# First expert slot of a routed layer cut into parts of 128 and 224 rows, with the narrow part's second layer turned

## Chip, core and metric

The kernel runs on one core of a Trainium2 chip. The metric is device time in microseconds (us), the median of several executions. The engines named below are TensorE (PE; PEld is its weight load, which overlaps PE), VectorE (DVE), ScalarE (ACT), GpSimd (POOL) and SyncE (SP), which issues most DMAs.

## Reference

Three blocks follow each other: local plus pooled attention, a routed layer with one expert per token, and a dense layer with a piecewise quadratic activation. The change touches the second block only.

```python
# x: attention output, 2304 tokens x 512
logits = x @ w_gate                     # 8 experts
expert_idx = np.argmax(logits, axis=1)  # one expert per token
for e in range(8):
    mask = expert_idx == e
    h = np.maximum(x[mask] @ w1[e], 0.0)        # 512 -> 1024
    out[mask] = gate_w[mask, None] * (h @ w2[e])  # 1024 -> 512
# then: h = out @ w_in; g = quadratic(h); result = g @ w_out   (512 -> 2048 -> 512)
```

All of it is to come out in float32 precision. The kernel therefore splits each operand into a rounded high part (`hi`, `wh`, `hh`, `xh`) and the rest (`lo`, `wl`, `hl`, `xl`), and each product is the sum of three passes: high by high, high by low, low by high.

## The kernel before, in words

Attention, gating and the scattering of the tokens to a DRAM table by expert (`xs_d`) come first and follow an order written out by hand (`ORDER`). Then eight *slots* run one after the other, the fullest expert first. A slot has 8 steps `f`, one for each 128 of the 1024 hidden features. A step has two products. `emit_p1` (the first product) has one weight block of 128 features stationary and the tokens as moving columns, and leaves a 128 x tokens block of hidden values in PSUM; ACT applies ReLU and rounds (`hh`), DVE makes the rest (`hl`). `emit_p2` (the second product) adds that block's share to four PSUM banks `y0` to `y3`, each holding 128 of the 512 outputs by tokens; its stationary operand is again a weight block and the tokens move. Each product of a full slot is 12 matmuls. The program emits the first product of step f+1 ahead of the second of step f.

Slot 0 has room for 416 tokens, but its expert is known before all tokens are scattered: the first rows of that expert are loaded early (`ld_rows`). So slot 0 starts with a *part A* of 144 tokens, while the rest of the routing is still being worked out. In A the first product is 4 matmuls of 288 columns (`hi` and `lo` of the tokens side by side) and 4 of 144. A runs steps 0 to 5; then the other tokens are fetched, turned (`x_rest`) and split; *part B*, the other 208 (or up to 272) tokens, runs steps 0 to 5 with the same weights; then all tokens run steps 6 and 7 together, 352 columns wide. `by_count` picks the narrow form (352 tokens in all) by the expert's count, and the traced execution took it. I write A0, B0 and so on for steps of the parts.

Weights come in tiles of 128x1024: tile 2j holds the first layer's weights of steps 2j and 2j+1, tile 2j+1 those of the second layer. SP loads a tile into one of four raw buffers (`load_wt`, issued by `wload`, L172), ACT rounds it to `wh` (`whi`, L181), DVE makes `wl` (`wlo`, L185), and that frees the raw buffer. For part A these three are placed by hand: `wh_`, `wd_` and `load_wt`, `wd_` inside `emit_p1` (its argument `mid`). From then on `next_wt` converts the next tile and issues the load of another one when the table `WFIRST` says how many tiles should be converted after sequence step k. A transfer that SP must wait for blocks all that stand behind it on SP. `blank_rows` makes SP wait for a flag that `tables` computes on DVE; `load_rest` fetches the other tokens of slot 0; `load_x(1)` those of slot 1, whose transposes (`xT_parts`) stand on PE in two halves ahead of the last two second products of slot 0. `starts`, `positions` and `emit_places` are bookkeeping on DVE that must run somewhere in slot 0.

Of the kernel before, what the change touches and what calls it, by code (L numbers as in the profile page):

```python
# [9 lines left out]
F32 = mybir.dt.float32  # L10
# [3 lines left out]
AF = mybir.ActivationFunctionType  # L14
ALU = mybir.AluOpType
# [4 lines left out]
B, H, S, D = 4, 8, 576, 64  # L20
# [12 lines left out]
CAP = 384  # L33
# [3 lines left out]
YCOLS = NT + CAPS[0]  # L37
NEG = -8.0e9
NWB, NWC, NWR = 3, 4, 4
NA, GA, FA, TOP = 144, 3, 6, 4096  # L40
NWT = NWB + NWC
NGR = 4
CONV0 = 8
WSTEP = (2, 1, 2, 1, 1, 1, 0, 0)
WFIRST = (0, 0, 0, 6, 6, 7, 8, 9, 10, 11, 11, 12, 13, 14)
PAT_MIN = float(np.array(0x38100000, np.uint32).view(np.float32))

C_ID = 0
# [72 lines left out]
def body(ctx: ExitStack, tc: tile.TileContext, qT, kT, kD, vS, wg, w1, w2, w_in, w_out, cst, out, dbg=None, parts="all"):  # L121
    nc = tc.nc
    PE, ACT, DVE, POOL, SP = nc.tensor, nc.scalar, nc.vector, nc.gpsimd, nc.sync
# [11 lines left out]
    def bank(tag):  # L135
        return ps.tile([128, 512], F32, tag=tag, name=tag)
# [3 lines left out]
    def next_bank(tag):  # L140
        turn[tag] += 1
        return bank(f"{tag}{turn[tag] % 2}")

    ident = const.tile([128, 128], F32, tag="ident", name="ident")
# [21 lines left out]
    wcount = [0]  # L166
# [37 lines left out]
    wts, wsrc, wpend = {}, [(s, k // 2, k % 2) for s in range(E) for k in range(8)], []  # L204

    def load_wt(after=None):
        if wsrc:
            s, j, second = wsrc.pop(0)
            if s < E:
                src, shp = slot_src(s, j, second)  # L210
            else:
                src, shp = w_out_src(wout_s, j) if second else w_in_src(win_s, j)
            wpend.append((s, wload(src, shp, after)))
# [44 lines left out]
    held = {}  # L258
# [391 lines left out]
    first = {}  # L650
# [60 lines left out]
    def wd_(eng, i):  # L711
        wlo(eng, *first["w", i])
# [188 lines left out]
    hb, yb = [None, bank("s1")], []  # L901
# [14 lines left out]
    for j in range(F2 // 256):  # L916
        for c in range(2):
            src = (w_in.bitcast(I32) if wide else w_in)[256 * c:256 * c + 256, :]
            n = 512 if wide else 256
# [100 lines left out]
    def split_psum(src, n, func_relu, hi, lo):  # L1020

        if func_relu:
            ACT.activation(out=hi, in_=src, func=AF.Relu)  # L1023
            DVE.scalar_tensor_tensor(out=lo, in0=src, scalar=0.0, in1=hi.bitcast(F32), op0=ALU.max, op1=ALU.subtract)  # L1024
        else:
            ACT.copy(out=hi, in_=src)
            DVE.tensor_tensor(out=lo, in0=src, in1=hi.bitcast(F32), op=ALU.subtract)
# [23 lines left out]
    def x_rest():  # L1051
        xr, m = first["xr"], (CAPS[0] - 128 - NA) // 2
        n = CAPS[0] - NA
        for c in range(4):
            p_ = next_bank("o")
            for t, c0, k in ((0, 0, 128), (2, 128, m), (3, 128 + m, m)):
                PE.transpose(out=p_[:, c0:c0 + k], in_=xr[0:k, t, 128 * c:128 * c + 128], identity=ident[0:k, 0:k])
            hi, lo = first["x"][c]
            split_psum(p_[:, 0:n], n, False, hi[:, NA:], lo[:, NA:])
            if c % 2:  # L1060
                yield

    PASSES = ((0, 0), (0, 1), (1, 0))

# [9 lines left out]
    def emit_p1(v, f, xhl, mid=None):  # L1074
        s, b, cap, _ = part(v)
        h_ps = hb[(f + 1) % 2]
        w = wts[s][2 * (f // 2)]

        def products(b, m):
            n = 0  # L1080
            for wi, xi in PASSES if f else (PASSES[0], PASSES[2], PASSES[1]):
                for c in range(4):
                    o = 256 * c + 128 * (f % 2)
                    PE.matmul(out=h_ps[:, b:m], lhsT=w[wi][:, o:o + 128], rhs=xhl[c][xi][:, b:m],  # L1084
                              start=(n == 0), stop=(n == 11))
                    n += 1

        hi = hp.tile([128, CAPS[0]], F32R, tag="hh", name="hh")
        lo = hp.tile([128, CAPS[0]], F32R, tag="hl", name="hl")
        if v == "A":  # L1090
            hv = h_ps[:, 0:2 * NA].rearrange("p (i n) -> p i n", i=2)
            for i in range(2):
                for c in range(4):
                    o = 256 * c + 128 * (f % 2)
                    PE.matmul(out=hv[:, 0] if i else hv, lhsT=w[i][:, o:o + 128], rhs=xhl[c][:, 0] if i else xhl[c],
                              start=(i == 0 and c == 0), stop=(i == 1 and c == 3))
            t = hp.tile([128, CAP], F32, tag="r", name="r", bufs=2)[:, 0:NA]
            ACT.copy(out=t, in_=hv[:, 1])
            DVE.tensor_tensor(out=t, in0=hv[:, 0], in1=t, op=ALU.add)
            ACT.activation(out=hi[:, 0:NA], in_=t, func=AF.Relu)  # L1100
            if mid is not None:
                wd_(DVE, mid)
                if mid > 2:
                    load_wt()
            DVE.scalar_tensor_tensor(out=lo[:, 0:NA], in0=t, scalar=0.0, in1=hi[:, 0:NA].bitcast(F32), op0=ALU.max, op1=ALU.subtract)
            return hi, lo
        by_count(v, products)
        split_psum(h_ps[:, b:cap], cap - b, True, hi[:, b:cap], lo[:, b:cap])
        return hi, lo

    def emit_p2(v, f, hl, y_ps):
        w = wts[part(v)[0]][2 * (f // 2) + 1]

        def products(b, m):
            for c, i in hi_first(4, 1):
                wi, xi = PASSES[i]
                o = 512 * (f % 2) + 128 * c
                PE.matmul(out=y_ps[c][:, b:m], lhsT=w[wi][:, o:o + 128], rhs=hl[xi][:, b:m],  # L1118
                          start=(f == 0 and i == 0 and v not in ("A", "B")), stop=(f == 7 and i == 1))

        by_count(v, products)

# [65 lines left out]
    def clear(t, stop):  # L1188
        PE.matmul(out=t[:, 0:CAPS[0]], lhsT=onesb, rhs=zerob.to_broadcast([128, CAPS[0]]), start=True, stop=stop)
# [2 lines left out]
    hl = emit_p1("A", 0, xhl, 2)  # L1192
    hb[0] = bank("s0")
    clear(hb[0], True)
    seq = [("A", f) for f in range(FA)] + [("B", f) for f in range(FA)] + [(0, f) for f in range(FA, 8)]
    for k, (v, f) in enumerate(seq):
        if k == FA - 1:
            xb = x_rest()
            next(xb)
            emit_p2(v, f, hl, yb)  # L1200
            next(xb)
            xhl = first["x"]
            hln = emit_p1(*seq[k + 1], xhl)
        elif k + 1 < len(seq):
            hln = emit_p1(*seq[k + 1], xhl, k + 2 if 0 < k < 4 else None)
            if f == 6:
                xTs = xT_parts(sx)
                next(xTs)
            if k == 0:
                yb.extend(bank(f"y{c}") for c in range(4))  # L1210
                for t in yb:
                    clear(t, False)
            emit_p2(v, f, hl, yb)
        else:
            next(xTs)
            emit_p2(v, f, hl, yb)
            emit_y(0, yb)
            xhl = next(xTs)
            sx = load_x(2)
            hln = emit_p1(1, 0, xhl)  # L1220
        hl = hln
        if k < 3:
            wh_(k + 3)
        while k > 2 and wcount[0] < WFIRST[k] and wpend:
            next_wt()
        if k == 0:
            tables()
            blank_rows()
            load_rest()
            load_wt()  # L1230
        elif k == FA - 2:
            load_n(0)
            starts()
        elif k == FA - 1:
            positions()
            actx.close()
            rest_pools()
            for c in range(4):
                POOL.memset(yT[c][:, NT:], 0.0)
        elif k == FA:  # L1240
            inner_pools()
            for c in range(4):
                for i, copy in enumerate((ACT.copy, POOL.tensor_copy)):
                    copy(out=first["x"][c][i][:, 0:NA], in_=first["xa"][c][:, i])
        elif k == FA + 3:
            sx = load_x(1)
        if k == len(seq) - 3:
            load_off(0)
            load_n(1)
        if 7 <= k < 14:  # L1250
            emit_places(k - 7)
    for e in range(1, E):
        y_ps = yb
        for f in range(8):
# [195 lines left out]
```

## Time and profile before

| | us |
|---|---|
| median of 3 executions | 760.73 (758.19 to 761.08) |
| profiled execution, its own time | 756.73 |
| its span in the trace | 755.0 |
| first matmul of part A to first matmul of slot 1 | 116.64 to 160.34 |
| PE busy over the span | 731.9 (97%) |

The profile gives the busy time of each engine, the waits with what ended them, a timeline with the start of each group of instructions, and the DMA issues. The start-to-start distance of matmuls in the timeline is what one costs when PE is full; the duration of one is longer, because they are pipelined.

### The profile page before, as it was taken

How to read it: one execution, taken by the hardware profiler on the slowest of the kernel's cores; microseconds unless marked ns; L12 is line 12 of the kernel's file. 1: busy time of each engine (PE TensorE's matmuls, PEld its weight loads, DVE VectorE, ACT ScalarE, POOL GpSimd, SP SyncE). 2: the span in 40 equal slices, each digit the busy share in tenths (PEclk: the TensorE clock that was granted, in tenths of full speed). 3: DMA queues.
4: the chain of work that ended last, by engine and by line, in shares of the span. 5: the costliest groups of instructions: out<-in, count | busy, mean ns of one | idle time of the engine just before them, and what ended most of it. 6: DMA issues, size and time to landing. Idle time of an engine off the chain costs nothing.

```text
span 755.0 us, 14570 instructions
## 1 busy us (share of the span) xinstructions
PE 731.9 (97%) x5647; PEld 660.5 (87%) x5648; DVE 527.7 (70%) x915; ACT 343.8 (46%) x719; POOL 257.5 (34%) x245
## 2 busy tenths in 40 slices
PE   5799999999999999999999999999999999999996
PEld 2577678999999999999899999999999989898986
DVE  5899977764668679664766766876867768644454
ACT  1777775453546556653554443333333333322221
POOL 5645653100143253001566633333333333111113
PEclk9999999999999999999999999999999999999999
DMA  9889266654556677650101010101010100011112
GB/s 287 250 288 285 99 202 211 217 191 146 171 204 205 209 233 224 202 166 4 57 28 55 31 57 28 57 29 57 28 56 29 56 0 1 1 43 42 43 43 84
DMA packets 47826, 87.12 MB, mean 115 GB/s; under 512 B 3092, under 2 KB 23956, under 8 KB 47744
## 3 DMA queue, kind: packets, MB, share of 16 engines
q1 hardware_dynamic: 44864, 76.56, 31.4%
q0 software_dynamic: 2880, 9.44, 3.3%
q8 instruction: 55, 0.90, 0.5%
q14 instruction: 27, 0.22, 0.1%
HBM read 76.55 MB, written 9.44 MB: 114 GB/s over the span
## 4 chain that ended last, share of the span: by engine, by line
PE 46%; issue 4%; POOL 2%; DVE 0%; POOLq 0%; ACT 0%; ACTq 0%
PE s L1168 23%; PE y L1326 15%; PE o L1326 8%; POOL out_dram L1346 1%; POOLq L1445 0%; POOL gap_t L1348 0%; DVE oacc L1344 0%; ACT r L1174 0%; DVE r L1175 0%; DVE r L1176 0%; DVE hl L1181 0%; ACT hh L1180 0%; POOLq L1346 0%; ACTq L1174 0%
## 5 line engine op out<-in xcount | busy, mean ns | idle before, releaser
L1168 PE MATMUL s<-yT,wh 128*128 128x384 f32 x448 | 140.5, 337 | 0.0
L980 POOL TENSOR_SCALAR cvm<-cvm 128x512 f32<-128x512 f32 x32 | 52.8, 1650 | 225.2 <-ACT cvm L979 224.8
L1180 ACT CAST hh<-r 128x384 fp32r<-128x384 f32 x95 | 48.8, 513 | 160.5 <-DVE r L1176 160.5
L1175 DVE SCALAR_TENSOR_TENSOR r<-r 128x384 f32<-128x384 f32 x96 | 61.9, 645 | 65.9 <-ACT r L1174 64.4
L1174 ACT ACTIVATE r<-s,half 128x384 f32<-128x384 f32 x96 | 55.8, 581 | 88.9 <-PE s L1168 87.5
L1181 DVE TENSOR_TENSOR hl<-r,hh 128x384 fp32r<-128x384 f32 x95 | 57.0, 600 | 55.2 <-ACT hh L1180 54.0
L185 DVE TENSOR_TENSOR wl<-wraw,wh 128x1024 fp32r<-128x1024 f32 x64 | 80.9, 1278 | 15.7 <-ACT wh L181 15.6
L1168 PEld LDWEIGHTS s<-yT,wh 128*128 128x128 f32 x448 | 83.5, 188 | 4.8 <-DVE yT L1158 0.2
L1168 PE MATMUL s<-yh,wh 128*128 128x384 f32 x256 | 86.3, 337 | 0.0
L1168 PE MATMUL s<-yh,wl 128*128 128x384 f32 x256 | 86.2, 337 | 0.0
L955 POOL TENSOR_TENSOR wl<-cvm,wh 128x512 fp32r<-128x512 f32 x32 | 50.9, 1591 | 98.5 <-ACT wh L954 87.4
L1118 PE MATMUL y<-hh,wh 128*128 128x240 f32 (+7 forms) x280 | 76.3, 297 | 0.5 <-ACT hh L1100 0.5
L1118 PE MATMUL y<-hh,wl 128*128 128x240 f32 (+7 forms) x280 | 75.1, 293 | 0.1
L1326 PE MATMUL y<-wl,hh 128*128 128x512 f32 x189 | 74.4, 393 | 0.0
L1326 PE MATMUL y<-wh,hh 128*128 128x512 f32 x189 | 73.9, 391 | 0.0
L181 ACT CAST wh<-wraw 128x1024 fp32r<-128x1024 f32 x64 | 65.7, 1045 | 4.6 <-issue 4.6
L1023 ACT ACTIVATE hh<-s 128x272 fp32r<-128x272 f32 (+7 forms) x64 | 27.2, 425 | 79.4 <-PE s L1084 79.3
L1326 PE MATMUL y<-wh,hl 128*128 128x512 f32 x189 | 59.3, 392 | 0.0
L1024 DVE SCALAR_TENSOR_TENSOR hl<-s,hh 128x272 fp32r<-128x272 f32 (+7 forms) x64 | 30.2, 471 | 40.2 <-ACT hh L1023 39.9
L1176 DVE TENSOR_TENSOR r<-s,r 128x384 f32<-128x384 f32 x96 | 53.5, 557 | 3.3
L1118 PEld LDWEIGHTS y<-hh,wh 128*128 128x128 f32 x280 | 53.0, 189 | 1.0 <-ACT hh L1100 1.0
L1118 PEld LDWEIGHTS y<-hh,wl 128*128 128x128 f32 x280 | 53.0, 189 | 0.3 <-DVE wl L185 0.3
(333 smaller groups left out, 1646.3 us busy)
## 6 DMA issues: line engine op xcount, KB each, us to landing
wraw<-in_dram SPq DMA_DIRECT2D x88, 512.0 KB, 3.7
v_s<-in_dram SPq DMA_DIRECT2D x12, 512.0 KB, 9.9
kbd<-in_dram SPq DMA_DIRECT2D x16, 296.0 KB, 8.3
kraw<-in_dram SPq DMA_DIRECT2D x4, 1152.0 KB, 5.9
craw<-in_dram SPq DMA_DIRECT2D x8, 512.0 KB, 4.5
q_t<-in_dram SPq DMA_DIRECT2D x4, 768.0 KB, 8.5
xr<-xs_d SPq DMA_DIRECT2D x9, 256.0 KB, 3.5
q_t<-in_dram SPq DMA_DIRECT2D x4, 400.0 KB
```

Source lines behind the costliest of these rows:

```text
L181: ACT.copy(out=hi, in_=raw)
L185: eng.tensor_tensor(out=lo, in0=raw, in1=hi.bitcast(F32), op=ALU.subtract)
L955: POOL.tensor_tensor(out=lo, in0=m, in1=hi.bitcast(F32), op=ALU.subtract)
L980: POOL.tensor_scalar(out=m, in0=m, scalar1=PAT_MIN * PAT_MIN, scalar2=None, op0=ALU.is_ge)
L1118: PE.matmul(out=y_ps[c][:, b:m], lhsT=w[wi][:, o:o + 128], rhs=hl[xi][:, b:m], start=(f == 0 and i == 0 and v not in ("A", "B")), stop=(f ...
L1168: PE.matmul(out=h_ps[:, 0:CAP], lhsT=w[wi][:, o:o + 128], rhs=yhl[j, c][xi], start=(n == 0), stop=(n == 11))
L1174: ACT.activation(out=r, in_=h_ps[:, 0:CAP], func=AF.Relu, scale=0.5, bias=half[:, 0:1])
L1175: DVE.scalar_tensor_tensor(out=r, in0=r, scalar=1.0, in1=r, op0=ALU.min, op1=ALU.mult)
L1176: DVE.tensor_tensor(out=r, in0=h_ps[:, 0:CAP], in1=r, op=ALU.max)
L1180: ACT.copy(out=hi[:, 0:CAP], in_=r)
L1181: DVE.tensor_tensor(out=lo[:, 0:CAP], in0=r, in1=hi[:, 0:CAP].bitcast(F32), op=ALU.subtract)
L1326: PE.matmul(out=p, lhsT=gl[gi][:, 128 * t:128 * t + 128], rhs=w[wi][:, o + c:o + c + p.shape[-1]], start=(f % 4 == 0 and i == 0), stop=(f ...
```

## The change

`NA` becomes 128 and `FA` 8: part A has 128 tokens and runs all eight steps, part B has 224 (or up to 288) and runs all eight, and the two joint steps are gone. A's first product is 12 matmuls of 128 columns. A's second product is turned (`emit_p2_rows`): the hidden block is stationary and the weights move, so 3 matmuls of 512 columns add to one PSUM bank `ya` that holds 128 tokens by 512 outputs. After A7, ACT copies `ya` to SBUF and four PE transposes put it into columns 0 to 127 of `y0` to `y3`, which are cleared there and no longer at A1. The ReLU and the rest of an A block are now one ACT and one DVE instruction in place of two and two. `x_rest` takes the four `y` banks in place of two others in turn, and is no longer split around a second product. `wh_` runs at steps 0 to 4 and `wd_` with a `load_wt` at each of the first six calls in part A, so tiles 0 to 7 are converted by hand; the load of tile 6 now stands ahead of `blank_rows` and `load_rest` on SP, and so does that of tile 7. `WFIRST` asks for nothing at steps 6 to 9 and for two tiles at step 10 (B2). `starts` and the later bookkeeping move by one to two steps, `load_x(1)` stays at the end of B3, and the copies of A's split tokens into the joint tiles (L1244) are gone.

```diff
-NA, GA, FA, TOP = 144, 3, 6, 4096
+NA, GA, FA, TOP = 128, 3, 8, 4096
-WFIRST = (0, 0, 0, 6, 6, 7, 8, 9, 10, 11, 11, 12, 13, 14)
+WFIRST = (0, 0, 0, 0, 0, 0, 8, 8, 8, 8, 10, 11, 11, 12, 13, 14)
@@ x_rest
-            p_ = next_bank("o")
+            p_ = yb[c]
...
-            if c % 2:
-                yield
@@ emit_p1
-        if v == "A":
-            hv = h_ps[:, 0:2 * NA].rearrange("p (i n) -> p i n", i=2)
...
-            ACT.copy(out=t, in_=hv[:, 1])
-            DVE.tensor_tensor(out=t, in0=hv[:, 0], in1=t, op=ALU.add)
-            ACT.activation(out=hi[:, 0:NA], in_=t, func=AF.Relu)
-            if mid is not None:
-                wd_(DVE, mid)
-                if mid > 2:
-                    load_wt()
...
+        ACT.activation(out=hi[:, b:cap], in_=h_ps[:, b:cap], func=AF.Relu)
+        DVE.scalar_tensor_tensor(out=lo[:, b:cap], in0=h_ps[:, b:cap], scalar=0.0, in1=hi[:, b:cap].bitcast(F32), op0=ALU.max, op1=ALU.subtract)
+        if mid is not None:
+            wd_(DVE, mid)
+            load_wt()
         return hi, lo
+
+    def emit_p2_rows(f, hl, ya):
+        w = wts[0][2 * (f // 2) + 1]
+        for n, (wi, xi) in enumerate(((0, 0), (1, 0), (0, 1))):
+            PE.matmul(out=ya, lhsT=hl[xi][:, 0:NA], rhs=w[wi][:, 512 * (f % 2):512 * (f % 2) + 512],
+                      start=(f == 0 and n == 0), stop=(f == 7 and n == 2))
@@ main sequence
-    seq = [("A", f) for f in range(FA)] + [("B", f) for f in range(FA)] + [(0, f) for f in range(FA, 8)]
+    ya = bank("o1" if held["n",] != "o1" else "o0")
+    seq = [("A", f) for f in range(FA)] + [("B", f) for f in range(FA)]
     for k, (v, f) in enumerate(seq):
         if k == FA - 1:
-            xb = x_rest()
-            next(xb)
-            emit_p2(v, f, hl, yb)
-            next(xb)
+            yb.extend(bank(f"y{c}") for c in range(4))
+            x_rest()
+            emit_p2_rows(f, hl, ya)
+            ya_sb = first["xr"][:, 1, :]
+            ACT.copy(out=ya_sb, in_=ya)
             xhl = first["x"]
             hln = emit_p1(*seq[k + 1], xhl)
+            yb[:] = [bank(f"y{c}") for c in range(4)]
+            for c, t in enumerate(yb):
+                clear(t, True)
+            for c, t in enumerate(yb):
+                PE.transpose(out=t[:, 0:NA], in_=ya_sb[:, 128 * c:128 * c + 128], identity=ident)
...
-        if k < 3:
+        if k < 5:
             wh_(k + 3)
...
         if k == 0:
             tables()
+        elif k == 1:
             blank_rows()
             load_rest()
-            load_wt()
...
         elif k == FA + 3:
             sx = load_x(1)
```

## Rows read from the trace of the kernel before

**Rows 1.** The page: busy time, share of the span and instructions of each engine.

```profile
PE 731.9 (97%) x5647; PEld 660.5 (87%) x5648; DVE 527.7 (70%) x915; ACT 343.8 (46%) x719; POOL 257.5 (34%) x245
```

**Rows 2.** Timeline, part A's beginning: start, duration, engine, line, operation, idle before.

```profile
116.64 0.84 PE L1095 MATMUL s<-hi,wh 128*128 128x288 f32 x4
...
118.12 1.30 ACT L775 ACTIVATE xr<-y,gt 128x512 f32<-128x512 f32 x2 [1.70 <-DVE rk L619]
...
118.86 0.94 PE L1189 MATMUL y<-zerob,onesb 128*128 128x416 bf16 x4
...
120.33 0.34 PE L1118 MATMUL y<-hh,wh 128*128 128x144 f32 x1 [0.53 <-ACT hh L1100]
...
122.11 0.16 DVE L726 SCALAR_TENSOR_TENSOR key<-o,keyb 128x8 f32<-128x8 f32 x1
...
124.09 0.16 DVE L745 TENSOR_REDUCE flag_i<-fl 1x1 int32<-1x16 f32 x1
...
124.39 1.20 DVE L185 TENSOR_TENSOR wl<-wraw,wh 128x1024 fp32r<-128x1024 f32 x1
...
125.65 0.33 PE L1118 MATMUL y<-hh,wl 128*128 128x144 f32 x1
```

**Rows 3.** Timeline, one undisturbed A step, with ACT, DVE, and SP at load_rest.

```profile
126.53 1.04 ACT L181 CAST wh<-wraw 128x1024 fp32r<-128x1024 f32 x1
...
126.79 0.37 SPq L858 DMA_DIRECT2D xr<-xs_d  x1
...
126.93 0.74 PE L1095 MATMUL s<-hi,wh 128*128 128x288 f32 x4
...
127.96 0.28 PE L1118 MATMUL y<-hh,wh 128*128 128x144 f32 x1
...
128.87 0.32 ACT L1100 ACTIVATE hh<-r 128x144 fp32r<-128x144 f32 x1 [0.37 <-DVE r L1099]
...
129.30 0.73 PE L1095 MATMUL s<-hi,wh 128*128 128x288 f32 x4
...
129.89 0.30 DVE L1105 SCALAR_TENSOR_TENSOR hl<-r,hh 128x144 fp32r<-128x144 f32 x1
```

**Rows 4.** Timeline, from part A to B: x_rest, and first products of B0 to B2.

```profile
131.61 0.66 PE L1057 MATMUL o<-ident,xr 128*128 128x128 f32 x6
...
132.07 0.67 ACT L1026 CAST xh<-o 128x272 fp32r<-128x272 f32 x2 [0.57 <-PE o L1057]
...
135.97 0.61 PE L1084 MATMUL s<-xh,wh 128*128 128x208 f32 x4
...
138.65 0.61 PE L1084 MATMUL s<-xh,wh 128*128 128x208 f32 x4
```

**Rows 5.** Timelines: eight transposes, then 512 columns with hidden values stationary, as emit_p2_rows has.

```profile
115.18 1.07 PE L631 MATMUL y<-ident,xT 128*128 128x128 f32 x8
...
500.04 0.39 PE L1326 MATMUL o<-wl,hh 128*128 128x512 f32 x1
500.27 0.40 PE L1326 MATMUL o<-wh,hh 128*128 128x512 f32 x1
```

**Rows 6.** Timeline, slot 0's end: the joint steps, slot 1's rows and its first product.

```profile
147.09 1.22 DVE L185 TENSOR_TENSOR wl<-wraw,wh 128x1024 fp32r<-128x1024 f32 x1
...
149.52 0.41 SPq L870 DMA_DIRECT2D xr<-xs_d  x1
...
150.13 1.25 SPq L873 DMA_DIRECT2D xr<-xs_d  x2
...
152.62 0.81 PE L1084 MATMUL s<-xh,wh 128*128 128x352 f32 x4
...
153.93 0.81 PE L1084 MATMUL s<-xh,wl 128*128 128x352 f32 x4
...
155.37 0.64 PE L1037 MATMUL o<-ident,xr 128*128 128x128 f32 x4 [0.32 <-DMA xr<-xs_d]
...
160.34 0.82 PE L1084 MATMUL s<-xh,wh 128*128 128x360 f32 x4
```

**Rows 7.** Time from issue to landing of weight tiles, 100 to 165 us.

```profile
DMA to landing us min/median/max: 3.3/4.8/7.2
```

More of the change, by code (lines that the diff above doesn't have):

```diff
@@ L1083, in products @@
                     o = 256 * c + 128 * (f % 2)
-                    PE.matmul(out=h_ps[:, b:m], lhsT=w[wi][:, o:o + 128], rhs=xhl[c][xi][:, b:m],
-                              start=(n == 0), stop=(n == 11))
+                    x = xhl[c][:, xi] if v == "A" else xhl[c][xi][:, b:m]
+                    PE.matmul(out=h_ps[:, b:m], lhsT=w[wi][:, o:o + 128], rhs=x, start=(n == 0), stop=(n == 11))
                     n += 1
@@ L1089, in emit_p1 @@
         lo = hp.tile([128, CAPS[0]], F32R, tag="hl", name="hl")
-        if v == "A":
-            hv = h_ps[:, 0:2 * NA].rearrange("p (i n) -> p i n", i=2)
[L1092 to L1097, printed above, removed]
-            ACT.copy(out=t, in_=hv[:, 1])
-            DVE.tensor_tensor(out=t, in0=hv[:, 0], in1=t, op=ALU.add)
-            ACT.activation(out=hi[:, 0:NA], in_=t, func=AF.Relu)
-            if mid is not None:
-                wd_(DVE, mid)
-                if mid > 2:
-                    load_wt()
-            DVE.scalar_tensor_tensor(out=lo[:, 0:NA], in0=t, scalar=0.0, in1=hi[:, 0:NA].bitcast(F32), op0=ALU.max, op1=ALU.subtract)
-            return hi, lo
-        by_count(v, products)
-        split_psum(h_ps[:, b:cap], cap - b, True, hi[:, b:cap], lo[:, b:cap])
-        return hi, lo
+        by_count(v, products)
+        ACT.activation(out=hi[:, b:cap], in_=h_ps[:, b:cap], func=AF.Relu)
[3 more added lines that the diff above has]
+            load_wt()
+        return hi, lo
+    def emit_p2_rows(f, hl, ya):
[3 more added lines that the diff above has]
+                      start=(f == 0 and n == 0), stop=(f == 7 and n == 2))
     def emit_p2(v, f, hl, y_ps):
@@ L1118, in products @@
                 PE.matmul(out=y_ps[c][:, b:m], lhsT=w[wi][:, o:o + 128], rhs=hl[xi][:, b:m],
-                          start=(f == 0 and i == 0 and v not in ("A", "B")), stop=(f == 7 and i == 1))
+                          start=(f == 0 and i == 0), stop=(f == 7 and i == 1))
         by_count(v, products)
@@ L1194, in body @@
     clear(hb[0], True)
-    seq = [("A", f) for f in range(FA)] + [("B", f) for f in range(FA)] + [(0, f) for f in range(FA, 8)]
+    ya = bank("o1" if held["n",] != "o1" else "o0")
+    seq = [("A", f) for f in range(FA)] + [("B", f) for f in range(FA)]
     for k, (v, f) in enumerate(seq):
         if k == FA - 1:
-            xb = x_rest()
-            next(xb)
-            emit_p2(v, f, hl, yb)
-            next(xb)
+            yb.extend(bank(f"y{c}") for c in range(4))
[3 more added lines that the diff above has]
+            ACT.copy(out=ya_sb, in_=ya)
             xhl = first["x"]
             hln = emit_p1(*seq[k + 1], xhl)
+            yb[:] = [bank(f"y{c}") for c in range(4)]
[3 more added lines that the diff above has]
+                PE.transpose(out=t[:, 0:NA], in_=ya_sb[:, 128 * c:128 * c + 128], identity=ident)
         elif k + 1 < len(seq):
-            hln = emit_p1(*seq[k + 1], xhl, k + 2 if 0 < k < 4 else None)
-            if f == 6:
+            hln = emit_p1(*seq[k + 1], xhl, k + 2 if 0 < k < 6 else None)
+            if v == "B" and f == 6:
                 xTs = xT_parts(sx)
                 next(xTs)
[L1209 to L1213, printed above, removed]
+            if v == "A":
+                emit_p2_rows(f, hl, ya)
+            else:
+                emit_p2(v, f, hl, yb)
         else:
@@ L1221, in body @@
         hl = hln
-        if k < 3:
+        if k < 5:
             wh_(k + 3)
-        while k > 2 and wcount[0] < WFIRST[k] and wpend:
+        while wcount[0] < WFIRST[k] and wpend:
             next_wt()
@@ L1227, in body @@
             tables()
+        elif k == 1:
             blank_rows()
             load_rest()
-            load_wt()
         elif k == FA - 2:
             load_n(0)
+        elif k == FA - 1:
             starts()
-        elif k == FA - 1:
+        elif k == FA:
             positions()
@@ L1239, in body @@
                 POOL.memset(yT[c][:, NT:], 0.0)
-        elif k == FA:
+        elif k == FA + 1:
             inner_pools()
-            for c in range(4):
-                for i, copy in enumerate((ACT.copy, POOL.tensor_copy)):
-                    copy(out=first["x"][c][i][:, 0:NA], in_=first["xa"][c][:, i])
         elif k == FA + 3:
@@ L1249, in body @@
             load_n(1)
-        if 7 <= k < 14:
-            emit_places(k - 7)
+        if k > FA:
+            emit_places(k - FA - 1)
     for e in range(1, E):
```

## The prediction

> **What bounds the kernel now.** I read the shares of the engines first: PE is busy for 731.9 of 755.0 us [rows 1]. So a stall of another engine matters only where PE stands, and what PE does counts one to one. Next I cut the changed stretch out of the timeline by the first matmul of each part: A starts at 116.64 [rows 2], the fetching of B's tokens (x_rest) at 131.61, B1's first product at 135.97 [rows 4], slot 1 at 160.34 [rows 6]. That gives three segments of 14.97, 4.36 and 24.37, together 43.70 us. From slot 1 on, code, weights converted (14 tiles) and loads issued (18) are as before, so a shift at 160.34 should reach the end unchanged.
>
> Then I read the pace of PE as start-to-start distances. An A step runs from 126.93 to 129.30: 1.03 for the first product and 1.34 for the 12 matmuls of 144 columns of the second, 0.111 each [rows 3]. Two products of B take 138.65 - 135.97 = 2.68, 24 matmuls of 208 columns, again 0.112 each [rows 4]. At 352 columns it is (153.93 - 152.62)/8 = 0.164, at 512 it is 0.232 [rows 5, 6]. So up to some 208 columns a matmul costs the same whatever its width; the weight load beside it sets the pace. That is the lever: a second product of 3 wide matmuls costs 0.70 where 12 narrow ones cost 1.34, and 352-wide steps cost 1.96 a product where B's cost 1.34.
>
> The waits come last. PE shows few: 0.53 for the first hidden block at 120.33, a gap ahead of 125.65 in the middle of a second product, which ends with a weight's low part on DVE (124.39 + 1.20) [rows 2], and the rows of slot 1 from DRAM, 0.32 at 155.37 alone [rows 6].
>
> **PE's own work.** Segment 1, from A0 to x_rest, holds after the change eight first products of 12 x 0.111 = 1.33 and seven turned second products of 3 x 0.232 = 0.70, 15.5 us, plus one clear (0.2, from four in 0.94 [rows 2]) and 0.1 for counting. That is 15.8. Before it held six first products and five second ones, 12.9, five clears and the two waits. The form of the turned product, hidden values stationary and 512 columns moving, is that of rows 5, so I take 0.232 as measured, and 0.51 (0.39 of matmul plus a load of 0.117, 660.5 us over 5648 [rows 1], that nothing hides) only as the dear end, kept for a rival. 128 columns lie just below the 144 of rows 3; the dear end is 0.112, the cheap end the slope from 352 to 512 columns, (0.232 - 0.164)/160 = 0.43 ns a column, or 0.054.
>
> [...]
>
> Segment 2, from x_rest to B1: 12 transposes 0.92 (six in 0.46 [rows 4]), the turned A7 0.70, B0's first product 1.34, four clears moved here 0.8, four transposes of A's result 4 x 0.113 = 0.45 ((1.07 - 0.28)/7 [rows 5]). The four casts of x take 0.34 each [rows 4] from 0.5 on, so the fourth is ready at 2.0 where PE wants it at 1.95: 0.1. The copy of `ya` on ACT follows them, ends by 2.7 and hides behind B0's first product and the clears, which last until 3.9; uncovered it would cost 0.6. Sum 4.3, against 4.36. The gain of 0.64 from the turned A7 and of some 0.7 from four banks in place of two in turn pays for the moved clears and the new transposes.
>
> [...]
>
> Segment 3, B1 to slot 1: fifteen products at 1.34 (224 columns; dear end 0.118 by the line through 208 and 352, then +1.0), 20.1, plus 1.2 for 12 transposes of slot 1 at the 0.08 to 0.11 of rows 4 and 5. Before: eleven at 1.34, four at 1.96, 1.2 of transposes and 0.6 of waiting (PE was through with its last 352-wide first product at 152.62 + 1.96 = 154.58 and went on at 155.37 with two of six transposes done [rows 6]), together 24.4. PE's own work so falls by 2.4 here, and over all three segments by nothing: +2.6 for A's products in segment 1, -0.64 and +0.45 in segment 2, -2.4 here; the clears only move.
>
> **What waits are added.** In A the lead of PE meets the conversions. ACT first finishes two scalings at 118.12 + 1.30 [rows 2], ReLU takes 0.32 [rows 3], so A0's hidden block is there at 119.8 and PE, done with A1's first product at 119.5, waits 0.3. DVE then has in its order: rest of A0 0.30, low part of tile 2 1.21, rest of A1 0.30, the table work 2.14 (122.11 to 124.25), rest of A2, low part of tile 3. That ends at 125.0, hardly sooner than the 125.6 before. PE reaches the second matmul of A2's turned product, which reads that tile, at 119.8 + 0.8 + 2 x 1.33 + 0.70 + 0.23 = 124.2: a wait of 0.8, and A3's first product, the hidden block of A3 and the rounding of tile 5 are queued behind it. Later the rest of A5 and the low part of tile 6 come one after the other (ReLU to 129.4, 0.3, 1.21: 130.95), and A6's first product wants that low part for its last four matmuls at 130.45: 0.5. Tiles 4, 5 and 7 come in time by 0.1 or more. Segment 1: 15.8 + 1.6 = 17.4, so +2.4; x_rest at 134.0.
>
> On SP the loads of tiles 6 and 7 now wait for these low parts (121.2 and 125.0) ahead of `blank_rows` and `load_rest`, and these so start up to 1.5 us later than at 126.79 [rows 3]; taking 4.8 like a weight tile [rows 7] they land by 133.2, ahead of 134.0. Nothing, and if they are late, what they are late by. Tile 7 lands at 125.0 + 4.8 = 129.8 by the median, when ACT wants it; by the slowest, 7.2, at 132.2, which holds ACT and DVE and costs 1.4.
>
> At the end of slot 0 the wait grows. `load_x(1)` stands on SP behind a load that waits for tile 10's low part. Before, that ended at 147.09 + 1.22 = 148.31, 1.6 after B5's first product began (138.65 + 6 x 1.34 = 146.7); the first rows were issued at 149.52, 1.2 later, the last at about 150.8, and PE's transposes went on at 155.37, 4.6 after that [rows 6]. After, two tiles are converted in B2 and one in B3. From the start of B3's first product: 1.34 and an estimated 0.6 to the end of ReLU (0.32 for 144 columns [rows 3], and its start), 1.04 rounding, 2.4 for two low parts, 1.0 for bookkeeping and the next rest, 1.2, less some 0.2 where instructions overlap, 7.4, of which four products are 5.4: 2.0 after B5's start, 0.4 later than before. And PE comes sooner: from B5's first product to the transposes it has five products of 1.34, 6.7, where it had three of 1.34 and two of 1.96, 7.9. So the wait is 0.6 + 1.2 + 0.4 = 2.2, and segment 3 is 20.1 + 1.2 + 2.2 = 23.5, against 24.4. No DMA is added; each removed instruction on ACT, DVE and POOL (the copies of A's tokens, A's extra copy and add) is off PE's path and gives nothing by itself.
>
> **Sum.** 17.4 + 4.3 + 23.5 = 45.2 against 43.7: +1.5 us. On the profiled execution's own 756.73 (the span and 1.7 around it, which stay) that is 758.2. This execution lies 4.0 below the median 760.73 of the three others; on the median's footing it is 762.2.
>
> **Rivals.**
> 1. *Slot 1's rows come in time.* If SP reaches `load_x` sooner (tiles 8 and 9 have long been loaded when B2 converts them), the wait of 2.2 goes: -0.7, 760.0. Against it: SP serves in order, and the low part of tile 10 is in DVE's order behind two others. 0.14.
> 2. *The conversions are not late in A*, since DVE's table work is 0.9 earlier still: the 0.8 and 0.5 go, +0.2, 760.9. 0.06.
> 3. *Narrow matmuls are cheaper*, paced by their columns: then A is paced by DVE, whose rests, low parts and tables sum to 11.5 from 119.8; segment 1 is 15.3 and B's products save 0.7. With slot 1's rows in time as well it is -3.5, 757.2. Rows 3 and 4 speak against it. 0.08, of which 0.05 below the bound for faster.
> 4. *Slower: slot 1's rows land late.* They share the queues with two weight tiles issued within 3 us before them. A transfer that takes 7.2, as the slowest tile [rows 7], and not some 4.6 adds 2.6: +4.1, 764.8. It decides from a landing of 6.9 us after issue on. 0.15.
> 5. *The turned product doesn't do what it says*: with its weight load uncovered it is 1.53 and not 0.70, eight times 0.83, +8.1, 768.8. Rows 5 speak against it. 0.05.
>
> **How the numbers follow.** My forecast has 0.52. A measurement of this kernel can tell about 0.5%, 3.8 us, from no change. Forecast, rivals 1 and 2 and the rest of 3 lie within it: 0.75. Slower is rivals 4 and 5, 0.20; faster 0.05. The range reaches from -2.0 (rivals 1 and 2 together) to +4.1 (rival 4), and some 0.8 of scatter between runs at either end: 758.0 to 765.6. The dear ends of the matmuls (+1.0) and the late tile 7 (+1.4) lie inside it.
>
> **What would show it.** A steps 2.0 apart in the timeline, turned matmuls 0.23 apart; two waits of PE for `wl` (L185) in A, near 124 and 130.5; x_rest at 134; waits for `xr` from DRAM of about 2 us ahead of slot 1, whose first product starts near 161.8. It is wrong if slot 1 starts before 159 or after 164, and the segment that differs says which term.

## The result and the profile after

The changed kernel is slower: 765.11 us (median of five, 764.04 to 766.36) against 760.73, a ratio of 1.0066 with a 95% interval of 1.0044 to 1.0088. Three later comparisons on three chips, each beside the kernel before, gave 1.0037 (1.0019 to 1.0055), 1.0047 (1.0032 to 1.0061) and 1.0045 (1.0027 to 1.0063). The forecast was no change, at 762.2; the time is inside the range given, near its upper end, and every interval lies on the slow side of 1.

The page's line on the engines, to be read beside [rows 1]. PE is busy for 3.7 us more, with four instructions more, though its work was to net to nothing. Matmuls at the lower clock, of which the windows below tell, count as longer busy (0.41 for one of 224 columns at 163.21, 0.27 at 157.20 ahead of it):

```profile
PE 735.6 (96%) x5651; PEld 662.8 (87%) x5652; DVE 526.6 (69%) x911; ACT 342.1 (45%) x712; POOL 254.9 (33%) x241
```

Timeline of after, that is, of the changed kernel, for part A and the step to B (start, duration, engine, line, operation, idle before), beside [rows 2 to 4]:

```profile
120.66 0.70 PE L1083 MATMUL s<-hi,wh 128*128 128x128 f32 x4
...
126.05 0.39 PE L1099 MATMUL o<-wl,hh 128*128 128x512 f32 x1
126.28 0.39 PE L1099 MATMUL o<-wh,hl 128*128 128x512 f32 x1
...
127.79 0.45 PE L1099 MATMUL o<-wh,hh 128*128 128x512 f32 x1
128.35 0.50 PE L1099 MATMUL o<-wl,hh 128*128 128x512 f32 x1
128.42 0.37 SPq L172 DMA_DIRECT2D wraw<-in_dram  x1
...
131.03 1.00 PE L1083 MATMUL s<-hi,wh 128*128 128x128 f32 x8
...
132.32 0.45 PE L1099 MATMUL o<-wh,hh 128*128 128x512 f32 x1
...
133.07 1.00 PE L1083 MATMUL s<-hi,wh 128*128 128x128 f32 x8
133.79 0.35 SPq L858 DMA_DIRECT2D xr<-xs_d  x1
134.31 0.66 PE L1083 MATMUL s<-hi,wl 128*128 128x128 f32 x4 [0.24 <-DVE wl L185]
...
137.99 1.20 PE L1057 MATMUL y<-ident,xr 128*128 128x128 f32 x12 [0.23 <-DMA xr<-xs_d]
...
142.16 0.68 PE L1083 MATMUL s<-xh,wh 128*128 128x224 f32 x4
```

A steps stand 2.04 apart (131.03 to 133.07), turned matmuls 0.23 apart (126.05 to 126.28). PE stumbles in three places: 127.79 to 128.35 where 0.29 is usual (it waits for the low part of tile 3), 133.07 to 134.31 where 0.85 is usual (low part of tile 6), and ahead of x_rest.

Timeline of after at the end of slot 0, beside [rows 6]:

```profile
153.63 1.22 DVE L185 TENSOR_TENSOR wl<-wraw,wh 128x1024 fp32r<-128x1024 f32 x1
...
156.09 0.41 SPq L870 DMA_DIRECT2D xr<-xs_d  x1
...
156.53 0.61 PE L1083 MATMUL s<-xh,wl 128*128 128x224 f32 x4
156.72 0.90 SPq L873 DMA_DIRECT2D xr<-xs_d  x2
...
159.21 0.61 PE L1083 MATMUL s<-xh,wl 128*128 128x224 f32 x4
161.00 0.32 PE L1037 MATMUL o<-ident,xr 120*128 120x120 f32 x1 [1.18 <-DMA xr<-xs_d]
161.63 0.32 PE L1037 MATMUL o<-ident,xr 112*128 112x112 f32 x1 [0.31 <-DMA xr<-xs_d]
162.25 0.75 PE L1037 MATMUL o<-ident,xr 128*128 128x128 f32 x4 [0.31 <-DMA xr<-xs_d]
162.66 0.54 PE L1109 MATMUL y<-hh,wh 128*128 128x224 f32 x1
...
163.21 0.41 PE L1109 MATMUL y<-hh,wh 128*128 128x224 f32 x1
163.42 0.41 PE L1109 MATMUL y<-hh,wl 128*128 128x224 f32 x1
...
167.65 0.84 PE L1083 MATMUL s<-xh,wh 128*128 128x360 f32 x4
```

And the same stretch by windows of 2 us (length, busy time of PE, PEld, DVE, ACT and POOL, granted clock of TensorE, DMA share, GB/s):

```profile
160.00:162.00 2.00, 0.64 (x2) 0.28 (x2) 0.93 (x2) 0.27 (x1) 0.00 (x0) 1.00 0.85 262
162.00:164.00 2.00, 1.75 (x10) 1.75 (x11) 0.89 (x2) 1.38 (x3) 0.00 (x0) 0.66 0.37 138
164.00:166.00 2.00, 2.00 (x12) 2.00 (x11) 1.60 (x3) 0.45 (x1) 0.00 (x0) 0.50 0.03 8
166.00:168.00 2.00, 2.00 (x19) 2.00 (x18) 1.47 (x5) 1.24 (x4) 0.00 (x0) 0.98 0.58 201
```

PE is through with B7's first product at 159.66 (159.21 and four times 0.112). It then has nothing but two small transposes until 162.25. Right behind this wait the granted clock is 0.50 for 3.4 us: 224-column matmuls now stand 0.21 apart (163.21 to 163.42) and not 0.112.

The stretch from A's first product to slot 1's is 46.99 us, where it was 43.70. From there to the end of the span it is 594.65 (762.3 - 167.65) against 594.66 (755.0 - 160.34): the shift reaches the end unchanged. The rest of the difference between these two profiles is that A starts 4.0 later, at 120.66. That is no part of the change: over all profiles taken here A starts at 117.6 to 122.2 in kernels with the change and at 116.6 to 121.5 in those without (last section).

### The profile page after: what moved, and what is told of

The parts are those of the page before. It is cut to its first block, busy times and chain, and to the rows that moved or that the text cites. A ratio compares the mean times of both kernels' runs of the same rounds, so it can differ in the third digit from the quotient of the medians.

```text
span 762.3 us, 14565 instructions
## 1 busy us (share of the span) xinstructions
PE 735.6 (96%) x5651; PEld 662.8 (87%) x5652; DVE 526.6 (69%) x911; ACT 342.1 (45%) x712; POOL 254.9 (33%) x241
## 4 chain that ended last, share of the span: by engine, by line
PE 45%; issue 4%; POOL 2%; DVE 0%; POOLq 0%; ACT 0%; ACTq 0%
PE s L1159 23%; PE y L1321 15%; PE o L1321 8%; POOL out_dram L1341 1%; POOLq L1440 0%; POOL gap_t L1343 0%; DVE oacc L1339 0%; ACT r L1165 0%; DVE r L1166 0%; DVE r L1167 0%; DVE hl L1172 0%; ACT hh L1171 0%; POOLq L1341 0%; ACTq L1165 0%
## 5 line engine op out<-in xcount | busy, mean ns | idle before, releaser
L1109 PE MATMUL y<-hh,wh 128*128 128x240 f32 (+5 forms) x256 | 70.7, 300 | 0.0
L1109 PE MATMUL y<-hh,wl 128*128 128x240 f32 (+5 forms) x256 | 69.4, 295 | 0.0
L1089 ACT ACTIVATE hh<-s 128x288 fp32r<-128x288 f32 (+7 forms) x72 | 29.3, 406 | 88.4 <-PE s L1083 88.4
L1090 DVE SCALAR_TENSOR_TENSOR hl<-s,hh 128x288 fp32r<-128x288 f32 (+7 forms) x72 | 32.3, 449 | 46.0 <-ACT hh L1089 45.7
L1159 PEld LDWEIGHTS s<-yh,wh 128*128 128x128 f32 x256 | 48.0, 188 | 2.9
L1109 PEld LDWEIGHTS y<-hh,wl 128*128 128x128 f32 x256 | 49.0, 191 | 0.0
```

The lines of the kernel that those rows point to most:

```text
L1159: PE.matmul(out=h_ps[:, 0:CAP], lhsT=w[wi][:, o:o + 128], rhs=yhl[j, c][xi], start=(n == 0), stop=(n == 11))
```

## Experiments

In every group the kernel before ran on the same chip, and a ratio in brackets compares with it. "Stretch" is A's first product to slot 1's. "The wait" is the time from the end of slot 0's last first product to the second product that follows, less 0.55 for the six transposes between them.

**The kernel before again**, two more profiles of the unaltered kernel.

> The kernel before, unchanged, for the clock of its single executions. In the traced execution of the changed kernel TensorE's granted clock was 0.50 from about 36.6 to 43.4 us, in the attention part, whose code is the same in both; part A's first matmul came 4.0 us later than in the trace of before (120.66 and 116.64). Theory 1: this fall belongs to neither kernel; some executions of before have it too, with a mean clock near 0.993 and times near 761, and those without it have 0.998 and about 757. Rival: the change brings it about, and every execution of before is near 0.998.

> The kernel before once more, for one profile: the stretch was 43.70 us in the profile shown ahead of the prediction and 42.59 in a second one. Theory: it lies between 42.5 and 43.8 again, with a wait of at most 0.7 us for slot 1's rows and no granted clock below 1 in the stretch.

Times 759.49 (ratio 1.0006, 0.9996 to 1.0017) and 761.64. The stretches are 42.59 and 43.92; with 43.70 the mean of three is 43.40. None has a granted clock below 1 in it: the windows of the first and third show 1.00 throughout, and in the second the matmuls at slot 1's rows keep their pace (352 columns 0.16 apart, 157.26 to 157.42). The third missed its expectation by a little: its wait is 0.96 (159.02 to 160.53, less 0.55), over the 0.7 expected, and its stretch is over 43.8.

**The changed kernel again**, five more profiles.

> The changed kernel, unaltered, beside the kernel before and the three others of this group, so that they share their conditions. Theory (the wait for slot 1's rows, and the fall of TensorE's granted clock behind it, are the whole of the loss): the stretch from A's first product to slot 1's is 46.5 to 47.2 us with a granted clock of 0.50 for some 3.4 us near the end of it, and the time is 4 to 5 us above that of the kernel before (ratio 1.005 to 1.0065). Rival (the loss seen lies in when the kernels happened to run, the stretch itself is only 1.5 us longer as forecast): ratio 1.002 and a stretch of 45.2.

> The changed kernel a third time, beside its own variant with early rows. Seen so far: with about the same wait of PE for slot 1's rows the granted clock fell to 0.50 behind it in one execution (stretch 46.99 us) and not in another (45.51 us). Theory (the wait of some 2 us is always there, the clock falls behind it in a part of the executions): a stretch of either 45.5 or 47.0 us and nothing between, and a time 1.5 to 4 us above the kernel before. Rival (the fall belongs to one chip): the stretch is 45.5, no granted clock below 1 there, and the time not more than 2.0 us above.

> The changed kernel once more, for one profile: the stretch is 45.5 us without a fall of the granted clock at slot 1's rows or 47.0 with one; which of the two is open.

> The changed kernel beside its variant with the wait filled, on one chip. In four profiles so far PE waited 2.4 to 3.2 us for slot 1's rows each time, and the granted clock fell to 0.50 behind it in two of the four, which cost 1.5 us each time. Theory (the wait always, the fall in about half of the executions): a stretch of 45.5 to 46.0 us without or 47.0 to 47.7 us with the fall, and a median some 0.8 us above that of the filled variant.

> The changed kernel for one more profile: 45.5 to 46.0 us from A to slot 1 without a fall of the granted clock there, 47.0 to 47.7 us with one.

Times 763.27, 764.64, 761.61 (one run), 764.50 and 762.99 (one run). Stretches of all six, the first included: 46.99, 45.51, 45.99, 47.68, 47.07, 47.22, mean 46.74, so 3.34 above the kernel before. The wait is in every one; the clock falls at it in four of six (all but 45.51 and 45.99). Two expectations missed: the first of the five had the fall as certain, and the second had nothing between 45.5 and 47.0, but the wait itself varies (2.72 in the one of 45.51, 3.25 in the one of 45.99). The rival that the fall belongs to one chip falls: it came on more than one chip, and on one chip in one profile of two. This is the second profile, without the fall:

```profile
159.44 0.32 PE L1037 MATMUL o<-ident,xr 120*128 120x120 f32 x1 [1.65 <-DMA xr<-xs_d]
159.99 0.32 PE L1037 MATMUL o<-ident,xr 112*128 112x112 f32 x1 [0.23 <-DMA xr<-xs_d]
160.50 0.64 PE L1037 MATMUL o<-ident,xr 128*128 128x128 f32 x4 [0.20 <-DMA xr<-xs_d]
160.90 0.35 PE L1109 MATMUL y<-hh,wh 128*128 128x224 f32 x1
...
161.20 0.28 PE L1109 MATMUL y<-hh,wh 128*128 128x224 f32 x1
161.31 0.27 PE L1109 MATMUL y<-hh,wl 128*128 128x224 f32 x1
...
164.28 0.84 PE L1083 MATMUL s<-xh,wh 128*128 128x360 f32 x4
```

Its wait was no shorter than the first's, yet its matmuls stay 0.11 apart. From the second product of B6 to slot 1 it needs 3.38 us (160.90 to 164.28); the first profile needs 4.99 (162.66 to 167.65), the fifth and sixth 4.88 and 4.93. So one fall costs 1.5 to 1.6 us behind the wait. The fourth profile needs 4.41 there, because its clock fell earlier, before PE had all the rows; its transposes are slowed with it (1.66 for five, 1.09 for the five of the variant one step less early, below):

```profile
159.57 1.66 PE L1037 MATMUL o<-ident,xr 112*128 112x112 f32 x5 [0.29 <-DMA xr<-xs_d]
```

```profile
159.00:160.00 1.00, 0.71 (x2) 0.26 (x2) 0.00 (x0) 0.00 (x0) 0.00 (x0) 0.81 0.67 242
```

**Slot 1's rows early**: the loading moved from `k == FA + 3` to `FA + 1`, where it is ahead of the weight loads that wait for conversions.

```diff
         elif k == FA + 1:
             inner_pools()
-        elif k == FA + 3:
             sx = load_x(1)
```

> The changed kernel with load_x(1) moved from the end of B3 to the end of B1, ahead of the two weight loads on SP that wait for DVE. In the changed kernel A's first matmul to slot 1's first product takes 46.99 us (before: 43.70), with a wait of 2.4 us for slot 1's rows and after it a granted clock of 0.50 for 3.4 us. Theory 1 (wait and clock): both go, the stretch is 46.99 - 2.4 - 1.7 = 42.9, the clock stays 1.00 there, and the time falls by 4.1 against the changed kernel, to about 761.0. Rival (the loss lies in part A, in more matmul work and late weight conversions; the rows only displace another wait): 45.5 to 47.

> The changed kernel with slot 1's rows loaded two steps earlier, a second time and now beside the changed kernel itself on one chip. Theory (wait and fall are the whole loss): a stretch of 43.2 us, no clock below 1 in it, the time within 1 us of the kernel before and 1.5 to 4 us below the changed kernel. Rival (some of the loss lies elsewhere): it stays 1.5 us or more above the kernel before.

Stretches of 43.23 and 43.22, times 759.07 (0.9994, 0.9980 to 1.0008) and 760.69 (0.9990, 0.9973 to 1.0008); in the second group the changed kernel itself stood at 764.64. The timeline and a window of the first:

```profile
158.72 0.61 PE L1083 MATMUL s<-xh,wl 128*128 128x224 f32 x4
159.16 0.79 PE L1037 MATMUL o<-ident,xr 120*128 120x120 f32 x6
...
163.41 0.82 PE L1083 MATMUL s<-xh,wh 128*128 128x360 f32 x4
```

```profile
158.00:160.00 2.00, 2.00 (x20) 2.00 (x20) 1.50 (x2) 0.66 (x3) 0.00 (x0) 1.00 0.04 14
```

All six transposes follow at once and PE has no idle time. Moving one load takes back the whole loss. What it takes away is the wait with whatever follows from it, so by itself it doesn't say which of the two weighs how much.

**One step less early**: `FA + 2` in place of `FA + 1`.

> The changed kernel with the loading of slot 1's rows one step earlier in the order (behind the second of the three last weight loads of slot 0, not behind the third), so that the rows are issued some 2 us sooner. Theory (a short wait costs itself alone, the clock falls only behind the long one): PE's wait for the rows shrinks from 2.45 to some 0.4, no granted clock below 1 there; the stretch is 46.99 - 2.05 - 1.6 = 43.3 us, the time within 0.2% of the kernel before. Rival (the clock falls there for what the new 224-column parts are, whatever the wait): the fall to 0.50 stays, and the stretch is 44.9 us, the time 1.9 us above the other.

Stretch 44.47, not 43.3; time 761.06 (1.0006, 0.9987 to 1.0025). PE was through at 158.73 and went on as follows, and behind that its 224-column matmuls stand 0.11 apart (161.16 to 161.27), as at the full clock:

```profile
159.44 0.32 PE L1037 MATMUL o<-ident,xr 120*128 120x120 f32 x1 [0.56 <-DMA xr<-xs_d]
160.13 1.09 PE L1037 MATMUL o<-ident,xr 112*128 112x112 f32 x5 [0.36 <-DMA xr<-xs_d]
160.97 0.35 PE L1109 MATMUL y<-hh,wh 128*128 128x224 f32 x1
```

The gap is 2.24 with six transposes in it, that take 0.55 (159.16 to 159.71 in the early variant): 1.7 of waiting and not 0.4. The rows were issued 2.0 sooner, counted from B1, but PE had the last of them only some 6.7 after the issue (153.83 to about 160.5), where it was 5.5 in the first profile. No fall here, as the theory says; but one profile is weak on this, since with the longer wait it stays away in two of six.

**The wait filled**: eight 512-column matmuls of no use behind B7's first product, so that PE works while it waits.

```diff
+                t = bank("o0")
+                for _ in range(8):
+                    PE.matmul(out=t, lhsT=onesb, rhs=onesb.unsqueeze(1).to_broadcast([128, 4, 128]), start=True, stop=True)
```

> The changed kernel with eight idle 512-column bf16 matmuls ahead of slot 1's first transposes, 1.7 us of work inside the wait of 2.4 us; the rows are loaded as late as before. Theory 1 (the wait lets the clock fall, and the fall costs 1.7 by itself): clock 1.00 through the end of slot 0, the stretch from A's first matmul to slot 1's first product 46.99 - 1.7 = 45.3, although more work is done. Rival (the clock has another cause, or costs nothing): 47.0 or more.

> The changed kernel with eight 512-column matmuls of no use in PE's wait for slot 1's rows, a second time and beside the changed kernel. Theory (PE's idling is what the clock falls for): no granted clock below 1 from A to slot 1, the stretch is 45.5 to 46.5 us (the wait for the rows stays), and the median is some 0.8 us below the changed kernel, half of what one fall costs. Rival (the fall has to do with something else there, the landing of the rows or the transposes): it falls here too, in about half of the looks.

> The variant with the wait filled for one more profile: no granted clock below 1 from A to slot 1, and a stretch of 45.5 to 46.5 us; by the rival, a fall in about half of such looks.

Stretches 46.53, 46.26 and 46.09; times 761.32 (1.0025, 1.0011 to 1.0039), 762.28 (1.0028, 1.0012 to 1.0044; the changed kernel beside it 764.50) and 762.28 (one run). Timeline and windows of the second:

```profile
158.31 1.90 PE L1207 MATMUL o<-onesb 128*128 128x512 bf16 x8
160.75 0.32 PE L1037 MATMUL o<-ident,xr 120*128 120x120 f32 x1 [0.54 <-DMA xr<-xs_d]
```

```profile
160.00:162.00 2.00, 0.87 (x4) 0.29 (x3) 0.00 (x0) 0.00 (x0) 0.00 (x0) 1.00 0.81 277
162.00:164.00 2.00, 2.00 (x18) 2.00 (x19) 0.97 (x2) 1.65 (x3) 0.00 (x0) 1.00 0.05 18
```

The wait is still there (158.31 to the second product at 162.38, less 0.55, is 3.5), but the clock falls in none of the three (the windows of the second and third show 1.00; in the first the 224-column matmuls stand 0.11 apart, 161.50 to 161.61), and the second product to slot 1 takes 3.38 or 3.39. Four of six against none of three is by itself a weak count. All 18 profiles of this document together, by their windows or the pace of their matmuls, are a stronger one: where PE idled for 2.45 us or more at these rows (the six of the changed kernel and the two variants below that hold the rows back or do not turn the product), the clock fell in six of eight; where it idled for less (1.9 at most, the 1.9 us of filling taken off), in none of ten. So in these profiles the clock stayed up where work took the place of idling. My 45.3 for the first of them was too low because I left the wait at 2.45, and it was 3.8 (156.99 to 161.31, less 0.55). The medians differ by 2.2 where I expected 0.8; the two groups of runs overlap, so the sign is likely and the size is not shown.

**The rows in the kernel before**, once two steps earlier, once held back behind a small write of VectorE.

```diff
-        elif k == FA + 3:
+        elif k == FA + 1:
             sx = load_x(1)
```

> The kernel before with the loading of slot 1's rows two steps earlier, so that PE should not wait for them. Theory (the two kernels are equal but for this wait): the 0.6 of waiting goes, the stretch is 42.0 to 43.1 us and the time 0.6 us lower, which is about the scatter of these runs. Rival (early rows take the queues from the weight tiles behind them, and a conversion is late): the stretch is as before or longer and PE waits for a low part of a tile in slot 0's second half.

```diff
+        if after:
+            after.memset(xr[:, :, 0:1], 0.0)
...
+        if k == FA + 5:
+            sx = load_x(1, DVE)
...
-        elif k == FA + 3:
-            sx = load_x(1)
```

> The kernel before with the loading of slot 1's rows held back: it stands two steps later and behind one small write of VectorE, that follows the hidden block of (0, 6); the rows should be issued some 3.0 us later than at 149.5. Nothing else of the change is in it. Theory (PE's wait makes the clock fall, in either kernel): the wait grows from 0.6 to some 3.6, the granted clock falls to 0.50 for some 3.4 us behind it, which costs a further 1.6; the stretch is 43.2 + 3.0 + 1.6 = 47.8 us and the time 4.6 us above the kernel before. Rival (the fall belongs to the narrow parts of the changed kernel): the clock stays at 1.00 and the stretch is 46.2 us, the time 3.0 above.

Early: stretch 42.79, time 759.67, ratio 0.9982 (0.9968 to 0.9996). This is the lowest ratio of all and below the kernel before, by little; its interval overlaps those of the changed kernel with early rows. Late: stretch 48.11 (47.8 expected), time 764.98, ratio 1.0040 (1.0024 to 1.0056). That is 3.0 us above the kernel before, as the rival had it, and not 4.6; the profiled execution was the slowest of its group (766.35), and one profile can't say in how many of the others the clock fell. Timeline and window of the late one:

```profile
158.61 0.80 PE L1086 MATMUL s<-xh,wl 128*128 128x352 f32 x4
160.73 0.29 PE L1039 MATMUL o<-ident,xr 120*128 120x120 f32 x1 [1.31 <-DMA xr<-xs_d]
...
163.12 0.94 PE L1039 MATMUL o<-ident,xr 128*128 128x128 f32 x4 [1.50 <-DMA xr<-xs_d]
```

```profile
164.00:166.00 2.00, 2.00 (x9) 2.00 (x8) 1.52 (x3) 1.41 (x2) 0.00 (x0) 0.50 0.00 0
```

With nothing of the change in it but a wait of this kind, the kernel before falls to the lower clock at the same place in this execution, as the theory had it. So here the fall comes behind a wait of 3.9 us and does not need the 224-column parts.

**A's second product not turned**: the part of 128 and 224 rows stays, its second layer is done in 12 narrow matmuls as before.

```diff
-                emit_p2_rows(f, hl, ya)
+                emit_p2(v, f, hl, yb)
```

> The changed kernel's split (128 and 224 rows, eight steps each) with part A's second product as before: 12 matmuls of 128 columns into the four y banks, no copy and no transposes of its result. My working: an A step costs 2.67 and not 2.03, 5.1 more in eight; the two waits for low parts (0.8 together) go because PE comes later, as do four transposes (0.45), two banks in turn cost 0.7: 4.5 us more than the changed kernel from A's first matmul to slot 1, 51.5. Rival (the turned product does not do what it says): within 1 us of the changed kernel's 47.0.

Stretch 52.73 (51.5 expected), time 767.66 (1.0116, 1.0092 to 1.0139). Its A steps:

```profile
128.21 1.06 PE L1085 MATMUL s<-hi,wh 128*128 128x128 f32 x8
...
130.89 1.06 PE L1085 MATMUL s<-hi,wh 128*128 128x128 f32 x8
```

They are 2.68 apart and not 2.04, so the turned product saves 0.64 a step, as 1.34 - 0.70 had it. Of the 5.7 by which its stretch is longer than that of after, 3.8 lie ahead of x_rest (21.10 against 17.33) and 1.9 behind B1 (27.44 against 25.49): its clock, too, fell at slot 1's rows, for some 6.8 us (0.50 in all windows from 164 to 170; matmuls 0.21 apart up to 169.97), and its wait for them was 3.5.

## Why the prediction was wrong

These are its three segments, as means of the six profiles after and the three before. The forecast column counts from the one profile before that the prediction had:

| segment | before | after | difference | forecast |
|---|---|---|---|---|
| A to x_rest | 14.61 | 17.22 | +2.61 | +2.4 |
| x_rest to B1 | 4.35 | 4.18 | -0.17 | -0.06 |
| B1 to slot 1 | 24.44 | 25.35 | +0.91 | -0.87 |
| sum | 43.40 | 46.74 | +3.34 | +1.5 |

**PE's own work: right.** The widths from 128 to 224 columns cost the same per matmul (0.108 at 128, 131.03 to 132.32 for 12; 0.112 at 224, 156.97 to 157.87 for eight), the turned product costs 0.75 a step (132.32 to 133.07; 0.70 was forecast) with its matmuls 0.23 apart, segment 2 is 4.18 where 4.3 was forecast. With the rows early in both kernels, what is left of the change is 43.23 - 42.79, +0.4; 0.3 of it are the second six transposes of slot 1, which take 0.83 there (161.14 to 161.97) and 0.55 in the second profile after. The sum without the two waits for rows was 45.2 - 2.2 against 43.7 - 0.6, or -0.1. Rivals 3 and 5 are out: 128 columns still take 0.11 (1.29 for the 12 from 131.03 on), and with turned matmuls 0.23 apart no weight load lies bare. That the weight load sets the pace of the narrow matmuls is the prediction's reading, and no run varied the load alone; in the trace of before the loads beside the 144-column matmuls stand 0.11 apart like these (128.01 to 128.79 for seven), in that of after those of the turned product 0.24 (132.37 to 132.61).

**The waits in A: near in sum, not in their parts.** The two for low parts are about 0.3 (0.56 less 0.29) and 0.4 (1.24 less 0.85), where 0.8 and 0.5 were forecast; rival 2, which had neither, came about half. The 0.3 for the first hidden block did not come (A1's first product is through at 123.56, and A0's second starts at 123.57). In their place comes one that I put at nothing: `load_rest` is issued at 133.79, 5.4 behind the load of tile 7, because SP first goes through `blank_rows` after it, and x_rest starts 0.4 late (137.36 to 137.99, where a turned matmul takes 0.23). The flag was ready by then (126.97); SP read it at 128.8 and needed 5.0 from there to `load_rest`, where before it needed 2.5 (124.3 to 126.79). Gaps between SP's own steps in `blank_rows` make up 2.9 of the 5.0 and 0.2 of the 2.5; in the other five profiles after they are 2.0 to 3.3, in the other two before 0.2. What makes them longer is open.

**The wait for slot 1's rows: right in its place, too small.** The order of events came as worked out: tile 10's low part ends at 154.85, 2.0 after B5's first product began (142.16 + 4 x 2.68 = 152.88), the rows are issued 1.2 later, PE is through 6.8 after B5 began. But PE went on 5.5 to 6.6 after the issue of the last pair of rows (156.72 to 162.25 in the first profile, 153.52 to 160.14 in the fourth), where before it was 5.2 (150.13 to 155.37 in [rows 6]) and 5.6 in the third profile before. So the wait is 2.45 in the first profile (159.66 to 162.66, less 0.55) and 2.7 to 3.25 in four others, not 2.2; in the fourth it is 3.85 (156.47 to 160.87, less 0.55), part of it transposes at the lower clock. This is rival 4 in small: late by 0.3 to 1.4, not by 2.6. Rival 1, no wait, did not come in any of the six.

**The step that failed: what the wait does to PE behind it.** I priced the wait at its length and took the products after it at their old pace. In four of six profiles the granted clock was 0.50 for some 3.4 us, and they ran at half their pace (0.21 apart and not 0.11 at 224 columns). Segment 3 is 24.15 and 24.68 without the fall, 25.49 to 26.31 with it, against a forecast of 23.5. So without the fall the segment was off by some 0.9, nearly all of it the longer wait (2.72 and 3.25, not 2.2); the fall adds 1.4 (25.82 less 24.42, means of four and two), 0.9 on average over the six. Both together are the 1.8 between +1.5 and +3.34. Neither the sum nor a rival had a term for it, though the prediction made PE wait for over 2 us at a place where it had idled for 0.96 at most in the three profiles before.

**The verdict.** +3.34 us is 0.44% of 760, and the four ratios lie around that (0.37 to 0.66%): the time went where the stretch says. To count from the median and not from the profiled execution's 756.73 was right: the medians of the kernel before are 759.02 to 761.25 in the later groups. What was missing moved the case from the middle of "within 0.5%" to its edge, and in the first comparison beyond it. That the time still lies in the range is partly luck: its upper end was set by rival 4, with rows 2.6 later, and neither end held a fall of the clock. By the prediction's own sign, slot 1 after 164, the miss is hardly seen: on the clock of the profile before, with A at 116.64, slot 1 starts at 163.4 on average and after 164 in the fourth profile alone. My chance of 0.20 for slower hung on a late landing and on a failing turned product, though the forecast itself stood at +1.5 and any further cost of its new waits went the same way.

## What to carry to other kernels

Price a new wait of the bounding engine at more than its length: look in the windows after it whether the granted clock falls, and add a term for it with a chance, because it comes in some executions and not in others (here in four of six profiles). When a part becomes shorter for the bounding engine, list every load that was timed by the old length; here one line that moves a load by two steps gives back all that the change lost. It gives no gain over the kernel before, though (ratios of 0.9994 and 0.9990), as PE's own work was not to change. A profile or two of each kernel is not enough where one of them has a clock event that comes and goes: compare the stretch over several.

## What the runs showed of the hardware

Among the longer waits the fall is not decided by their length alone. With a wait of 2.45 us it came, with one of 3.25 (third profile) it didn't; in the late variant of the kernel before, with 3.9 (158.61 + 4 x 0.164 = 159.27 to 163.72, less 0.55), it came. What decides in between stays open: no run here varied it.

A second place of this kind lies in attention, in code that both kernels share, where PE stops in the middle of a row of equal matmuls and waits for nothing that the profile shows ("issue"). The restart in after, and below it in before:

```profile
37.79 1.28 PE L371 MATMUL s<-kbd,q_t 128*32 128x64 f32 x37 [3.34 <-issue]
```

```profile
36.55 0.76 PE L371 MATMUL s<-kbd,q_t 128*32 128x64 f32 x37 [3.06 <-issue]
```

Behind it the window of after shows the lower clock, that of before does not:

```profile
38.00:40.00 2.00, 2.00 (x49) 1.83 (x43) 0.88 (x2) 0.50 (x1) 0.00 (x0) 0.50 0.29 56
```

```profile
36.00:38.00 2.00, 1.45 (x53) 1.29 (x53) 0.65 (x2) 1.51 (x4) 0.00 (x0) 1.00 0.08 26
```

In after it lasts 6.8 us. In the further profiles whose windows show attention the lower clock was there for 3.4 us (second, fourth and sixth of after, the second with the wait filled) or 6.8 us (third and fifth of after, the third with the wait filled, the third of before), in the fourth of after some 7 us earlier, and not at all in the second one with early rows. The profile of before that the prediction rests on is without it, its A starts earliest of all, and its 756.73 lay 4.0 under the median. The fall can't be the only reason for that: in the one with early rows A starts at 119.70 without it. Over all profiles A starts within 5.5 us (116.64 to 122.15), which is more than the change is worth.
